# Attention stage: relu of the next queries at a unit's head, row norms before the tail scores, router set-up after unit 0, zero rows sent by SyncE

## Chip, cores and metric

One core of a Trainium2 chip runs one program. The metric is the device time of one execution in microseconds (us); the median of several runs counts. TensorE (PE), VectorE (DVE), ScalarE (ACT), GpSimd (POOL) and SyncE (SP) each work through a queue of their own in order; semaphores tie them together.

## What is computed

Attention with a compressive memory, whose output feeds a routed mixture of experts and then a dense one. Only the first is touched by the change.

```python
# attention: B, H, S, D = 4, 8, 576, 64
scores = q @ k.T / sqrt(D), causal;  a = softmax(scores)
local = a @ v
q_p = phi(q)            # phi(x) = max(x, 0) + min(exp(x), 1)
mem_out = (q_p @ M_prev) / (q_p . z_prev + 1e-6)
g = sigmoid(beta);  out = g * mem_out + (1 - g) * local
# routed experts: N = 2304 tokens, 512 wide, 8 experts, 1024 hidden
e_idx = argmax(x @ w_gate + modality_bias[modality_id])
out[t] = gate_w[t] * (relu(x[t] @ w1[e_idx]) @ w2[e_idx])
# dense experts: all 8 experts on all tokens, weighted by a Sinkhorn-normalised matrix
```

## The kernel before

**Units.** The function `attention` works in 16 units of two heads each (`NU = B * NP`, four units to a batch row). A unit's queries and keys are five tiles of up to 128 rows (`NT`), the last half full. The whole loop stands in a manual schedule (line 349): every engine gets its instructions in the order in which the loop emits them, and it does not pass one that waits. Two units overlap: in the pass for unit u the scores and exponentials of u are made, and the transposes, the memory product and the product with V of unit u-1 (`ex`); the keys and queries of u+1 are transposed there too (`nx`).

**The order of a pass** (lines 372 to 450). SP issues the loads of V of u+1 and of Q and K of u+2. Then `phi_a(u)`: VectorE forms phi of the queries (line 136), GpSimd multiplies it by z (line 137). `finish(u-1)`: the exponential of the tail scores of u-1 on ScalarE (line 262), two small VectorE steps (267, 268) and a scaling on GpSimd (269). `high(u)`: the scores of tiles 3 and 2 on TensorE (line 229) and their masks (336); these matmuls are called the head of the unit below. `top(u, 3)`: VectorE takes the row maxima (line 246). The transposed probabilities of u-1 are then evicted one bank after the other by VectorE and ScalarE (`ptrans`, lines 284 to 303), in between come `exps` (260), `keys` (188), `queries` (195, 196), `inverse` (175, 181), `low` (229, 345) and `phis` (203). After `ptrans(u-1, 3)` follow `ptrans` 6 and 7 (lines 298, 299, 303), `tails` (210 to 218), `last_scores`, the tail's maximum (248), `gate_v(u)` on GpSimd (144), the row norms `phi_b(u)` (VectorE 151 to 154, GpSimd 156), `phi_c(u)` (VectorE 161, 163, 166; GpSimd 165, 168), and `phi_0(u+1)`: relu of the next queries on GpSimd (line 127) and their exponential on ScalarE (128). Last come `memory(u-1)` (312) and `av(u-1)` (324), whose results VectorE writes to `xT` (326).

**Banks.** The transposes and the two products share four PSUM banks in turn (`ps_t`), so a product of `memory` needs the bank that `ptrans` 3 or 6 filled to be evicted. The scores have two buffers (`ps_s`): `low` needs the one of tile 3.

**Router.** `Router(...)` (line 358) sets up constants and loads the gate's weights, the modality ids and the bias; it runs after unit 0's queries and ahead of the loop. `pad_gate` (line 491) clears a tile on GpSimd and then has ScalarE's queue issue its load. `rt.batch(g)` is a generator: `some()` takes one step of it at three places of a pass. Its steps make the logits of a batch row's tokens, their maxima and one-hot rows, the row numbers, and send the rows to `xs_sorted` by indirect DMA from GpSimd.

**Zero rows.** `rt.clear()` (line 553) runs at the head of unit 2: GpSimd clears `zrow`, and ScalarE's queue issues 16 DMAs of 256 KB from it to `xs_sorted`.

Of the kernel before, what the change touches and what calls it, by code (L numbers as in the profile page):

```python
# [23 lines left out]
DVE_PT = (0, 1, 3)  # L24


def attention(ctx, tc, q, k, v, M_prev, z_prev, beta, xT, ident, router=None):
    nc = tc.nc
    es = ctx
    c1 = es.enter_context(tc.tile_pool(name="at_c", bufs=1))  # L30
# [89 lines left out]
                              src[b, 2 * a:2 * a + 2, 512:, :].rearrange("h p d -> p h d"))  # L120
            ld[u, nm] = t

    def phi_0(u):

        ex = tmp.tile([128, NT, 128], F32, tag="ex", name="ex")
        qp = tmp.tile([128, NT, 128], F32, tag="qp", name="qp")
        (nc.gpsimd if u else nc.vector).tensor_scalar(qp, ld[u, "q"], 0.0, None, ALU.max)
        nc.scalar.activation(ex, ld[u, "q"], AF.Exp)
        ph[u] = ex, qp

    def phi_a(u):

# [216 lines left out]
    with tc.manual_schedule():  # L349
        load(0, "kq")  # L350
        load_b(0)
        load(0, "v")
        load(1, "kq")
        keys(0)
        queries(0)
        tails(0, None)
        phi_0(0)
        rt = router and router()
        if rt:
            rt.ps, rt.busy = ps_t, busy  # L360
            rt.table_parts()

        back = iter(())

        def some():
            next(back, None)

        def finish(u):
            exps(u, 4)
            norm(u)  # L370

        for u in range(NU + 1):
            go, ex, nx = u < NU, u > 0, u + 1 < NU
            if nx:
                load(u + 1, "v")
            if u + 2 < NU:
                if (u + 2) % NP == 0:
                    load_b((u + 2) // NP)
                load(u + 2, "kq")
            if u == 2 and rt:  # L380
                rt.clear()
            if go:
                phi_a(u)
                if ex:
                    finish(u - 1)
                high(u)
                top(u, 3)
            some()
            if ex:
                ptrans(u - 1, 5)  # L390
                ptrans(u - 1, 4)
            if go:
                exps(u, 3)
            if ex:
                ptrans(u - 1, 0)
            if go:
                top(u, 2)
                exps(u, 2)
            if ex:
                ptrans(u - 1, 1)  # L400
            if nx and ex:
                keys(u + 1)
                queries(u + 1)
            if ex:
                inverse(u - 1)
            if go:
                low(u)
            if ex:
                ptrans(u - 1, 2)
                phis(u - 1)  # L410
            if go:
                top(u, 1)
                top(u, 0)
            if ex:
                ptrans(u - 1, 3)
            some()
            if ex:
                ptrans(u - 1, 6)
                ptrans(u - 1, 7)
            if go:  # L420
                exps(u, 1)
                exps(u, 0)
            if nx and not ex:
                last_scores(u)
                keys(u + 1)
                queries(u + 1)
            if nx or ex:
                tails(u + 1 if nx else None, u - 1 if ex else None)
            if go:
                if ex:  # L430
                    last_scores(u)
                top(u, 4)
                gate_v(u)
                phi_b(u)
                phi_c(u)
            some()
            if nx:
                phi_0(u + 1)
            elif go:
                finish(u)  # L440
            if ex:
                memory(u - 1, 0)
                memory(u - 1, 1)
                av(u - 1, 0)
                av(u - 1, 1)
                if rt and u % NP == 0:
                    for _ in back:
                        pass
                    back = rt.batch(u // NP - 1, ps_t)
                del un[u - 1]  # L450
        for _ in back:
            pass
# [46 lines left out]
class Router:  # L499
# [50 lines left out]
        self.tab = [c.tile([128, 4], I32, name=f"tab{i}") for i in range(2)]  # L550
        self.num = c.tile([1, 2], I32, name="num")

    def clear(self):
        nc = self.nc
        z = self.wk.tile([128, DM], F32, tag="zrow", name="zrow", bufs=1)
        nc.gpsimd.memset(z, 0.0)
        for e in range(NE):
            for r in range(TB // 128):
                nc.scalar.dma_start(self.xs[e * N + r * 128:e * N + (r + 1) * 128], z)

    def batch(self, g, ps):
        nc, xT, wk = self.nc, self.xT, self.wk
        tiles = GROUPS[g]
        t0, T = tiles[0], len(tiles)
        lt = []
        for c0 in range(0, T, 4):
            n = min(4, T - c0) * 128
            lq = ps.tile([128, 512], F32, tag="t", name="lq")
            for kd in range(KD):
                nc.tensor.matmul(lq[kd * 32:(kd + 1) * 32, :n], self.wg[:, kd],  # L570
                                 xT[:, kd, (t0 + c0) * 128:(t0 + c0) * 128 + n], start=True, stop=True)
            lt.append(wk.tile([128, 512], F32, tag="lt", name="lt"))
            nc.vector.tensor_copy(lt[-1][:, :n], lq[:, :n])
        yield
        L = wk.tile([128, T, NE], F32, tag="L", name="L")
        mx = wk.tile([128, T], F32, tag="mx", name="mx")
        ex = wk.tile([128, T, NE], F32, tag="ex", name="exr")
        gate = wk.tile([128, T], F32, tag="gate", name="gate")
        km = wk.tile([128, T], F32, tag="km", name="km")

        def bc(a):
            return a[:, :, None].to_broadcast([128, T, NE])

        def bce(a):
            return a[:, None, :].to_broadcast([128, T, NE])

        for c0 in range(0, T, 4):
            n = min(4, T - c0)
            lp = ps.tile([128, n, KD, 32], F32, tag="t", name="lp")
            for t in range(n):  # L590
                nc.tensor.transpose(lp[:, t].rearrange("p k e -> p (k e)"), lt[c0 // 4][:, t * 128:(t + 1) * 128],
                                    self.ident)
            nc.vector.tensor_reduce(L[:, c0:c0 + n], lp[:, :, :, :NE].rearrange("p t k e -> p t e k"), AX.X, ALU.add)
        nc.vector.tensor_tensor(L, L, self.bias[:, t0:t0 + T], ALU.add)
        nc.vector.tensor_reduce(mx, L, AX.X, ALU.max)
        nc.vector.tensor_tensor(L, L, bc(mx), ALU.subtract)
        nc.scalar.activation(ex, L, AF.Exp)
        yield
        nc.vector.tensor_reduce(gate, ex, AX.X, ALU.add)
        nc.vector.tensor_scalar(gate, gate, 1e-9, None, ALU.add)  # L600
        nc.vector.reciprocal(gate, gate)
        nc.vector.scalar_tensor_tensor(L, L, 0.0, bce(self.e8), ALU.is_ge, ALU.mult)
        nc.vector.tensor_reduce(km, L, AX.X, ALU.max)
        oh = self.oh[:, t0:t0 + T]
        nc.vector.tensor_tensor(oh, bc(km), bce(self.e8), ALU.is_equal)
        yield

        rp = ps.tile([128, T, NE], F32, tag="t", name="rp")
        nc.tensor.matmul(rp, self.ones, bce(self.base1), start=True, stop=False)
        nc.tensor.matmul(rp, self.ones, bce(self.cum), start=False, stop=False)  # L610
        nc.tensor.matmul(rp, self.tri, oh, start=False, stop=False)
        for t in range(T - 1):
            nc.tensor.matmul(rp[:, t + 1:], self.ones, oh[:, t:t + 1].to_broadcast([128, T - 1 - t, NE]), start=False,
                             stop=(t == T - 2))
        nc.vector.tensor_tensor(L, rp, oh, ALU.mult)
        nc.vector.tensor_reduce(self.rowf[:, t0:t0 + T], L, AX.X, ALU.add)
        nc.vector.tensor_copy(self.row[:, t0:t0 + T], self.rowf[:, t0:t0 + T])
        if g + 1 < len(GROUPS):
            for t in range(T):
                nc.vector.tensor_tensor(self.cum, self.cum, oh[:, t], ALU.add)  # L620
        for t in tiles:
            if t > t0 and t % 2:
                yield
            xp = ps.tile([128, DM], F32, tag="t", name="xp")
            for kd in range(KD):
                nc.tensor.transpose(xp[:, kd * 128:(kd + 1) * 128], xT[:, kd, t * 128:(t + 1) * 128], self.ident)
            xr = wk.tile([128, DM], F32, tag="xr", name="xr", bufs=6)
            nc.scalar.activation(xr, xp, AF.Copy, scale=gate[:, t - t0:t - t0 + 1])
            scatter(self.tc, self.moved, self.gap, self.xs[:, :], self.row[:, t:t + 1], xr)
# [770 lines left out]
```

## Time and profile before

| what | us |
|---|---|
| median of 3 runs | 2122.35 |
| the runs | 2119.94 to 2122.36 |
| the profiled execution, its own time | 2123.79 |
| span of its trace | 2122.1 |
| TensorE busy in the span | 2029.5 (96%) |
| VectorE, ScalarE, GpSimd busy | 1472.3, 853.0, 774.5 |
| mean granted TensorE clock | 0.981 |

The span is what lies between the first and the last instruction; 1.7 us of the execution lie around it. Busy shares are means over stages with different limits: the attention stage takes the first 322 us or so, and the expert stages the rest. A line of the timeline gives the start, the busy time, the engine, the source line, what is written from what, and in brackets how long the engine had been idle and what ended that.

### The profile page before, as it was taken

To read this page: it belongs to the slowest core of one execution; us is meant where nothing else is said; L and a number is where in the kernel's file an instruction comes from. 1 tells how busy PE (TensorE), PEld (TensorE's weight loads), DVE (VectorE), ACT (ScalarE), POOL (GpSimd) and SP (SyncE) were. 2 spreads that over 40 slices of the span, in tenths; PEclk is the share of its full clock that TensorE was granted. 3 is DMA by queue.
4 is the path that set the end of the run, shared out by engine and by line. 5 is a ranking of instruction groups with operands and counts; after the bars stand their busy time and mean duration, and the time that the engine had idled before them with its cause. 6 is when DMAs were issued, how large, how long until landed. Compare 5 with 4: busy or idle time off the path is not lost.

```text
span 2122.1 us, 31397 instructions
## 1 busy us (share of the span) xinstructions
PE 2029.5 (96%) x11478; PEld 1789.2 (84%) x11480; DVE 1472.3 (69%) x2538; ACT 853.0 (40%) x1792; POOL 774.5 (36%) x758
## 2 busy tenths in 40 slices
PE   5788889999989999999999999999999999999998
PEld 3556667999869998899889898899988999889997
DVE  4567666766668777776687677766778676777775
ACT  3454554655543433333343433333334333333332
POOL 4354541000024334344465433334347343333432
PEclk8899999999999999999999999999999999999999
DMA  4332206665632223443433212122122221212211
GB/s 97 111 78 59 75 26 224 201 214 195 202 122 65 60 80 60 63 77 60 75 65 100 70 60 80 60 69 71 60 78 92 70 70 60 79 60 71 70 60 40
DMA packets 238525, 187.36 MB, mean 88 GB/s; under 512 B 71444, under 2 KB 194324, under 8 KB 238356
## 3 DMA queue, kind: packets, MB, share of 16 engines
q1 hardware_dynamic: 229012, 171.48, 29.3%
q0 software_dynamic: 3520, 9.46, 1.2%
q10 hardware_dynamic: 5824, 4.25, 0.6%
q8 instruction: 95, 1.56, 0.3%
q14 instruction: 74, 0.61, 0.1%
HBM read 171.51 MB, written 13.64 MB: 87 GB/s over the span
## 4 chain that ended last, share of the span: by engine, by line
issue 30%; PE 24%; POOL 17%; DVE 0%; ACT 0%; POOLq 0%; DVEq 0%
PE y L1202 12%; PE prod L1131 11%; POOL T L1023 8%; POOL w1l L1017 7%; POOL out_dram L477 1%; PE lq L1243 0%; POOLq L1023 0%; POOL S L1101 0%; POOL S L1103 0%; POOL S L1102 0%; DVE w2l L1017 0%; POOL S4l L1017 0%; POOL S L1100 0%; PE lg L1255 0%; DVE c L1145 0%
## 5 line engine op out<-in xcount | busy, mean ns | idle before, releaser
L1149 ACT ACTIVATE hh<-c 128x384 fp32r<-128x384 f32 x384 | 202.0, 526 | 829.8 <-DVE c L1145 829.7
L1017 POOL TENSOR_TENSOR w1l<-T,w1h 128x1024 fp32r<-128x1024 f32 x94 | 226.7, 2411 | 842.4 <-ACT w1h L1017 842.4
L1202 PE MATMUL y<-w2h,hh 128*128 128x512 f32 x1152 | 453.3, 394 | 0.0
L1202 PE MATMUL y<-w2l,hh 128*128 128x512 f32 x1152 | 453.3, 393 | 0.0
L1202 PE MATMUL y<-w2h,hl 128*128 128x512 f32 x1152 | 452.6, 393 | 0.0
L1154 DVE SCALAR_TENSOR_TENSOR hl<-c,hh 128x384 fp32r<-128x384 f32 x384 | 418.1, 1106 | 1.1 <-ACT hh L1149 0.8
L1145 DVE TENSOR_TENSOR c<-prod,u 128x384 f32<-128x384 f32 x288 | 160.2, 556 | 155.6 <-PE prod L1131 152.7
L1202 PEld LDWEIGHTS y<-w2h,hh 128*128 128x128 f32 x1152 | 216.2, 188 | 32.8
L1202 PEld LDWEIGHTS y<-w2h,hl 128*128 128x128 f32 x1152 | 216.2, 188 | 28.5
L1202 PEld LDWEIGHTS y<-w2l,hh 128*128 128x128 f32 x1152 | 216.3, 188 | 27.9
L1023 POOL TENSOR_TENSOR T<-r,T 128x256 f32<-128x256 f32 x188 | 159.1, 846 | 14.8 <-issue 7.7
L1023 POOL TENSOR_TENSOR T<-r 128x256 f32<-128x256 f32 x188 | 161.1, 857 | 7.1
L1145 DVE TENSOR_TENSOR u<-prod,u 128x384 f32<-128x384 f32 x192 | 106.0, 552 | 58.1 <-PE prod L1131 57.7
L1145 DVE TENSOR_TENSOR u<-prod,p 128x384 f32<-128x384 f32 x96 | 53.5, 557 | 129.5 <-PE prod L1131 128.3
L1017 DVE TENSOR_TENSOR w2l<-r,w2h 128x512 fp32r<-128x512 f32 x188 | 137.1, 729 | 0.6 <-ACT w2h L1017 0.6
L1017 ACT CAST w2h<-r 128x512 fp32r<-128x512 f32 x188 | 106.7, 610 | 0.0
L1017 DVE TENSOR_TENSOR w1l<-r,w1h 128x512 fp32r<-128x512 f32 (+1 forms) x188 | 103.9, 553 | 0.0
L1145 DVE TENSOR_TENSOR c<-prod,p 128x384 f32<-128x384 f32 x96 | 53.5, 558 | 71.1 <-PE prod L1131 65.2
L1017 ACT CAST w1h<-T 128x1024 fp32r<-128x1024 f32 x94 | 97.0, 1032 | 1.0 <-POOL T L1023 1.0
L1159 ACT COPY p<-prod 128x384 f32<-128x384 f32 x96 | 46.1, 480 | 123.8 <-PE prod L1131 122.5
L1213 DVE SCALAR_TENSOR_TENSOR acc<-y,P,acc 128x512 f32<-128x512 f32 x126 | 92.4, 744 | 4.3 <-PE y L1202 4.3
L1017 ACT CAST w1h<-r 128x512 fp32r<-128x512 f32 (+1 forms) x188 | 94.5, 503 | 0.0
(387 smaller groups left out, 4179.2 us busy)
## 6 DMA issues: line engine op xcount, KB each, us to landing
r<-in_moe_w_dram SPq DMA_DIRECT2D x188, 512.0 KB, 4.1
r<-in_moe_w_dram SPq DMA_DIRECT2D x188, 256.0 KB, 2.9
xr<-xs_sorted SPq DMA_DIRECT2D x22, 256.0 KB, 5.0
kn<-in_k_dram SPq DMA_DIRECT2D x32, 128.0 KB, 2.6
qn<-in_q_dram SPq DMA_DIRECT2D x32, 128.0 KB, 2.8
vt<-in_v_dram SPq DMA_DIRECT2D x32, 128.0 KB, 2.7
xs_sorted<-zrow ACTq DMA_DIRECT2D x16, 256.0 KB, 3.7
zb<-in_z_prev_dram SPq DMA_DIRECT2D x4, 256.0 KB
```

Of the source, the lines that this page charges most:

```text
L477: i = tc.nc.gpsimd.indirect_dma_start(out=out, out_offset=bass.IndirectOffsetOnAxis(ap=idx, axis=0), in_=src, in_offset=None)
L1017: return (lambda: nc.scalar.copy(hi, src)), (lambda: eng.tensor_tensor(lo, src, hi.bitcast(F32), ALU.subtract))
L1023: sub = lambda i, a, b: (lambda: nc.gpsimd.tensor_tensor(T[:, i], a, b, ALU.subtract))
L1131: nc.tensor.matmul(p, a[:, kd], b[:, kd], start=(i == 0), stop=(i == 5))
L1145: nc.vector.tensor_tensor(st[o], a, st[b], ALU.add)
L1149: nc.scalar.activation(hh[:, f, a * HT:(a + 1) * HT], st[o], AF.Relu)
L1154: nc.vector.scalar_tensor_tensor(hl[:, f, w], st[o], 0.0, hh[:, f, w].bitcast(F32), ALU.max, ALU.subtract)
L1159: nc.scalar.copy(st["p1"], p)
L1202: nc.tensor.matmul(yt[t], a[:, f, t * 128:(t + 1) * 128], b[:, f], start=(j == 0 and f == 0 and i == 0), stop=(j == NJ - 1 and f == 1 and ...
L1213: nc.vector.scalar_tensor_tensor(acc[t], yt[t], P[:, m, e:e + 1], acc[t], ALU.mult, ALU.add)
```

## The change

Seven edits, all in the attention stage and its router. (1) The relu of the queries leaves `phi_0(u+1)` at the end of pass u and stands at the head of pass u, behind `gate_v(u)`; its buffer gets a third copy. (2) Exponential (`phi_e(u+1)`) and `phi_a(u+1)` stand at the end of pass u, `phi_a` thus no longer at the head of pass u+1. (3) `gate_v(u)` moves from the end of pass u to its head. (4) `phi_b(u)` moves from behind `top(u, 4)` to behind `ptrans(u-1, 3)`, ahead of `ptrans` 6. (5) `phi_e(u+1)` stands ahead of `top(u, 4)`. (6) The router is set up at the end of pass 0, behind `phi_a(1)`. (7) The 16 zero DMAs are issued by SP, eight each behind the loads of units 1 and 2. The generator `batch` has one more empty step ahead of the row numbers.

```diff
+    def relu(u):
+        qp = tmp.tile([128, NT, 128], F32, tag="qp", name="qp", bufs=3)
         (nc.gpsimd if u else nc.vector).tensor_scalar(qp, ld[u, "q"], 0.0, None, ALU.max)
-        nc.scalar.activation(ex, ld[u, "q"], AF.Exp)
+        ph[u] = tmp.tile([128, NT, 128], F32, tag="ex", name="ex"), qp
+    def phi_e(u):
+        nc.scalar.activation(ph[u][0], ld[u, "q"], AF.Exp)
...
-        phi_0(0)
-        rt = router and router()
-            rt.table_parts()
+        relu(0)
+        phi_e(0)
+        phi_a(0)
...
-            if u == 2 and rt:
-                rt.clear()
+            if 0 < u < 3:
+                rt.clear(u - 1)
             if go:
-                phi_a(u)
+                gate_v(u)
+            if nx:
+                relu(u + 1)
+            if go:
                 if ex:
                     finish(u - 1)
                 high(u)
...
             some()
+            if go:
+                phi_b(u)
             if ex:
                 ptrans(u - 1, 6)
                 ptrans(u - 1, 7)
...
+            if nx:
+                phi_e(u + 1)
+            if go:
                 top(u, 4)
-                gate_v(u)
-                phi_b(u)
                 phi_c(u)
             some()
             if nx:
-                phi_0(u + 1)
+                phi_a(u + 1)
             elif go:
                 finish(u)
+            if u == 0:
+                rt = router()
+                rt.ps, rt.busy = ps_t, busy
+                rt.table_parts()
...
-    def clear(self):
+    def clear(self, part):
-        for e in range(NE):
+        for e in range(NE // 2 * part, NE // 2 * (part + 1)):
             for r in range(TB // 128):
-                nc.scalar.dma_start(self.xs[e * N + r * 128:e * N + (r + 1) * 128], z)
+                nc.sync.dma_start(self.xs[e * N + r * 128:e * N + (r + 1) * 128], self.z)
...
         nc.vector.tensor_tensor(oh, bc(km), bce(self.e8), ALU.is_equal)
         yield
+        yield
```

## Rows read from the trace of the kernel before

**Rows 1.** Windows, head to head of units; columns as the second line says.

```profile
core 0: us, PE busy (x) PEld busy (x) DVE busy (x) ACT busy (x) POOL busy (x), PEclk, DMA share, GB/s
...
26.91:45.36 18.45, 14.59 (x98) 11.26 (x98) 10.93 (x30) 8.16 (x25) 8.31 (x7) 0.81 0.01 2
45.36:76.90 31.54, 15.25 (x107) 10.98 (x103) 10.91 (x27) 9.52 (x29) 8.73 (x8) 0.73 0.53 174
94.04:110.98 16.94, 14.61 (x107) 10.77 (x103) 11.17 (x28) 8.92 (x27) 8.25 (x8) 0.90 0.24 54
110.98:129.18 18.20, 16.24 (x119) 11.56 (x115) 12.14 (x30) 9.18 (x28) 8.23 (x7) 0.91 0.22 50
129.18:148.31 19.13, 15.83 (x128) 11.48 (x124) 15.57 (x46) 10.99 (x31) 12.04 (x14) 1.00 0.40 109
76.90:310.00 233.10, 196.57 (x1419) 143.92 (x1417) 158.64 (x404) 122.37 (x364) 121.50 (x117) 0.93 0.25 62
310.00:2122.00 1812.00, 1788.81 (x9806) 1615.53 (x9804) 1279.05 (x2051) 703.84 (x1350) 627.16 (x583) 1.00 0.32 90
```

**Rows 2.** Waits in 0 to 345 us: who for whom, sum, times, longest.

```profile
DVE qp L136 <- POOL qp L127: 39.1, 15, 4.5
ACT P L262 <- DMA xs_sorted<-zrow: 18.5, 1, 18.5
SPq L117 <- PE x L324: 176.7, 13, 21.3
```

**Rows 3.** Timeline of unit 4, head at 94.04: start, us, engine, operation, idle before.

```profile
92.42 0.81 DVE L151 TENSOR_REDUCE nrm<-ex 128x10 f32<-128x640 f32 x1
...
93.81 0.17 DVE L161 TENSOR_SCALAR su<-su 128x8 f32<-128x8 f32 x1
...
94.38 0.81 DVE L326 TENSOR_TENSOR xT<-x,R 128x256 f32<-128x256 f32 x2
...
98.93 1.21 DVE L246 TENSOR_REDUCE nm<-s 128x2 f32<-128x1024 f32 x1
...
105.39 0.56 DVE L284 COPY pt<-tp 128x384 f32<-128x384 f32 x1 [0.40 <-PE tp L283]
...
106.39 0.21 DVE L213 COPY pT<-tl 128x64 f32<-128x64 f32 x1
...
106.98 1.22 PE L312 MATMUL x<-pT,Mb 128*128 128x256 f32 x4
```

**Rows 4.** Timeline of unit 2: the zero rows, its late head, its maxima.

```profile
50.10 11.75 ACTq L559 DMA_DIRECT2D xs_sorted<-zrow  x16
...
62.78 1.65 PE L229 MATMUL s<-kT,qTp 64*128 64x384 f32 x4 [16.29 <-ACT P L262]
...
64.80 1.23 DVE L246 TENSOR_REDUCE nm<-s 128x2 f32<-128x1024 f32 x1 [1.69 <-PE s L336]
```

**Rows 5.** Timeline of units 0 and 1, up to unit 1's phi.

```profile
8.75 0.53 ACTq L514 DMA_DIRECT2D ids<-in_moe_modality_id_dram  x1
...
9.31 0.40 PE L336 MATMUL s<-mk,idb 128*128 128x128 bf16 x4
...
13.06 0.18 DVE L519 CAST idf<-ids 128x18 f32<-128x18 int32 x1 [3.81 <-DMA ids<-in_moe_modality_id_dram]
...
15.95 2.09 DVE L246 TENSOR_REDUCE nm<-s 128x2 f32<-128x1024 f32 x2
16.00 1.53 POOL L137 TENSOR_TENSOR ex<-qp,zb 128x640 f32<-128x640 f32 x1 [8.91 <-DMA vt<-in_v_dram]
...
27.99 0.61 POOL L165 COPY rr<-rc 128x512 f32<-128x512 f32 x1
...
28.56 1.05 POOL L168 TENSOR_TENSOR qp<-qp,nrm 128x512 f32<-128x512 f32 x1
...
31.47 0.83 DVE L136 SCALAR_TENSOR_TENSOR qp<-ex,qp 128x640 f32<-128x640 f32 x1 [3.52 <-POOL qp L127]
```

**Rows 6.** Two VectorE operations by tile: duration ns min/median/max, first and last start.

```profile
L166 DVE TENSOR_TENSOR nrm<-nrm,su x16: 116/330/334, 27.6 to 310.6; 128x8 f32<-128x8 f32 x16
L1154 DVE SCALAR_TENSOR_TENSOR hl<-c,hh x384: 532/591/2551, 616.1 to 2106.0; 128x384 fp32r<-128x384 f32 x192
```

More of the change, by code (lines that the diff above doesn't have):

```diff
@@ L24, with attention @@
 DVE_PT = (0, 1, 3)
-def attention(ctx, tc, q, k, v, M_prev, z_prev, beta, xT, ident, router=None):
+def attention(ctx, tc, q, k, v, M_prev, z_prev, beta, xT, ident, router):
     nc = tc.nc
@@ L121, in load @@
             ld[u, nm] = t
-    def phi_0(u):
-        ex = tmp.tile([128, NT, 128], F32, tag="ex", name="ex")
-        qp = tmp.tile([128, NT, 128], F32, tag="qp", name="qp")
+    def relu(u):
+        qp = tmp.tile([128, NT, 128], F32, tag="qp", name="qp", bufs=3)
         (nc.gpsimd if u else nc.vector).tensor_scalar(qp, ld[u, "q"], 0.0, None, ALU.max)
-        nc.scalar.activation(ex, ld[u, "q"], AF.Exp)
-        ph[u] = ex, qp
+        ph[u] = tmp.tile([128, NT, 128], F32, tag="ex", name="ex"), qp
+    def phi_e(u):
+        nc.scalar.activation(ph[u][0], ld[u, "q"], AF.Exp)
     def phi_a(u):
@@ L356, in attention @@
         tails(0, None)
-        phi_0(0)
-        rt = router and router()
-        if rt:
-            rt.ps, rt.busy = ps_t, busy
-            rt.table_parts()
+        relu(0)
+        phi_e(0)
+        phi_a(0)
+        rt = None
         back = iter(())
@@ L445, in attention @@
                 av(u - 1, 1)
-                if rt and u % NP == 0:
+                if u % NP == 0:
                     for _ in back:
@@ L551, in __init__ @@
         self.num = c.tile([1, 2], I32, name="num")
-    def clear(self):
+    def clear(self, part):
         nc = self.nc
-        z = self.wk.tile([128, DM], F32, tag="zrow", name="zrow", bufs=1)
-        nc.gpsimd.memset(z, 0.0)
-        for e in range(NE):
+        if part == 0:
+            self.z = self.wk.tile([128, DM], F32, tag="zrow", name="zrow", bufs=1)
+            nc.gpsimd.memset(self.z, 0.0)
+        for e in range(NE // 2 * part, NE // 2 * (part + 1)):
             for r in range(TB // 128):
-                nc.scalar.dma_start(self.xs[e * N + r * 128:e * N + (r + 1) * 128], z)
+                nc.sync.dma_start(self.xs[e * N + r * 128:e * N + (r + 1) * 128], self.z)
     def batch(self, g, ps):
```

## The prediction

> **What bounds the kernel now.** I read the windows first. From 310 us on TensorE is busy for 1788.81 of 1812.00 us at full clock [rows 1], and nothing of the change reaches there: I carry that part over unchanged. Ahead of it TensorE is not the limit: units 3 to 15 take 233.10 us with 196.57 us of TensorE work, at a mean clock of 0.93 [rows 1]. A plain unit, without router work, takes 16.94 us with 14.61 us of TensorE at a clock of 0.90; at full clock that work would be some 13.1 us (14.61 x 0.90), my estimate. Then I read the waits: 15 times VectorE stands before phi (line 136) for GpSimd's relu, 39.1 us in all or 2.6 us a unit, and ScalarE stands once for 18.5 us behind the zero rows [rows 2]. The timeline shows why the first of these is on the path: in unit 4 the maxima of tile 3 start 4.89 us behind the head (98.93 against 94.04) [rows 3], and everything of the unit hangs on them: evictions, exponentials, the free score buffer. In unit 2, where the stall had let relu and phi pass before the head, they start 2.02 us behind it (64.80 against 62.78), waiting for the masks alone [rows 4].
>
> **A plain unit.** (Edits 1 to 5.) The relu goes to GpSimd's queue most of a unit earlier, and phi to the end of the pass before. VectorE's next work at the head is the maxima, at about head + 2.05 us (2.02 in unit 2). From there to the copy of the tail bank (line 213) unit 4 takes 7.46 us (98.93 to 106.39) [rows 3]. The norms now come in between: 1.39 us (92.42 to 93.81) [rows 3]. Of the gaps that VectorE had in this stretch 0.40 us stands ahead of the third eviction [rows 3]; with a maximum that starts earlier against the same TensorE order I close it and, by estimate, as much again: the smaller gaps ahead of the low tiles. So 7.46 + 1.39 - 0.78 = 8.07 us. From line 213 to the next head unit 4 takes 4.59 us (106.39 to 110.98) [rows 1, 3]. The first half of the memory product (0.6 of the 1.22 us of line 312 [rows 3]) no longer has to stand behind that, since its bank is the one of the third eviction: 4.0 us. Sum: 2.05 + 8.07 + 4.0 = 14.1 us.
>
> What is late next? First VectorE's end of the pass. The norms leave it (1.39 us), phi comes (0.83 us [rows 5]); the copies to `xT` ended at head + 1.15 us (94.38 + 0.81) [rows 3], so about 0.55 us remain to head + 2.05 (0.35 us of that I give to the two small steps of `finish`, which have room from the 0.56 us by which phi is shorter). Second, GpSimd: from the reciprocals at the end of a pass until the tail's scaling it has 7.85 us of work in a row (8.25 us busy a unit [rows 1], less some 0.4 for the early piece of the norms), and the tail's transposes want it at about head + 7.7 us: it fits with little over. Third, ScalarE: 8.92 us a unit [rows 1], no limit.
>
> A price that the trace of before does not show is that of phi (two inputs in SBUF) beside GpSimd's copy of the reciprocals and its scaling (0.61 and 1.05 us [rows 5]): before, phi ran when GpSimd had just finished its relu. Between nothing and both of them, 1.66 us, I take one, 0.61 us: line 166, the nearest row, has two such inputs and takes 0.33 us at the median against 0.116 at best [rows 6], so it is held, but by one instruction of GpSimd and not by a row of them. With the slack above that is 0 to 0.2 us on VectorE and, since GpSimd then starts its next piece 0.8 us late, about 0.3 us a unit in all. **14.4 us a plain unit**, with ends at 13.6 (TensorE's 13.1 and one wait) and 15.3 (phi held by both: 14.1 + 1.66 - 0.55 of slack, and 0.1 for GpSimd).
>
> The Trainium skill bears on this place. SBUF — State Buffer, section Who interferes with whom, says that a VectorE instruction with two SBUF inputs and a GpSimd instruction that reads SBUF take one port by turns, and that the second to issue blocks fully. The trace agrees in line 1154: 0.59 us at the median, 2.55 at the longest [rows 6]. By that rule alone, with GpSimd issuing first both times, a unit would be the 15.3 us of the upper end.
>
> **Router pieces.** Units 5 and 6 carry one batch: VectorE has 12.14 and 15.57 us of work against 11.17 in unit 4 [rows 1], together 5.4 us more. The one-hot part stays at the end of a pass, where there is a little room; the logits and the row numbers lie between the maxima and line 213, on the path. The empty step shifts the row numbers from a head to mid-pass and the last scatters into the following unit, whose tail scaling they delay. I take 4.9 us a batch, three batches: 14.7 us, give or take 5.
>
> **Units 3 to 15.** 13 x 14.4 + 14.7 = 201.9 us against 233.1: **31.2 us saved**.
>
> **Unit 2.** (Edit 7.) Its 31.54 us [rows 1] hold the stall: the zeros occupy ScalarE's queue for 11.75 us and its next exponential waits 18.5 us, with the head 16.29 us behind [rows 2, 4]. On SP they stand behind the loads of their unit, and the loads of the next unit wait for `av` anyway (13 waits, 176.7 us [rows 2]): eight DMAs, about 5.9 us of issue by half of 11.75, fit into that wait. If that cover were gone, the next loads would start up to 6 us late, once or twice, for data wanted a unit later. So unit 2 becomes a plain unit: 31.54 - 14.4 = **17.1 us saved**.
>
> **Units 0 and 1.** (Edit 6.) The maxima of unit 0 start at 15.95 us although its masks end at 9.71 [rows 5]: the set-up stands ahead of them. They can start at 10.0, some 5.9 us earlier. But the set-up now stands at the end of pass 0, in three queues. GpSimd's scaling, which ended at 29.61 (28.56 + 1.05), ends 5.9 us for the earlier start and 1.4 for the norms sooner, at 22.3; the product with z follows (1.53 us): 23.8; only then comes `pad_gate`'s memset, for which ScalarE's queue waits, with the ids behind it. Their load takes 4.31 us from issue to VectorE's cast (8.75 to 13.06), so the cast is at about 28.8, and VectorE's set-up (2 us) ends near 30.9. The maxima of unit 1 stand behind it: 31.0 us, against about 32.5 before (31.47 and phi's 0.83, then two small steps) [rows 5]. So of 5.9 us about 1.5 are left, less 0.2 for the norms on a colder clock: **1.3 us saved**, between 2 us lost (bias landing late) and 6 saved (nothing held).
>
> **Sum.** 31.2 + 17.1 + 1.3 = 49.6 us. On the profiled execution's own time: 2123.8 - 49.6 = 2074.2. That execution is 1.4 us above the median of the runs, so for the median: **2072.8 us**.
>
> **Rivals.**
> (a) GpSimd and its port set the pace. Phi is held by both GpSimd pieces in each unit, the tail scaling comes late: 15.3 us a unit, 14 x 0.9 = 12.6 us less saved, 2085. For it: 7.85 us in a row, and line 1154's longest of 2.55 us [rows 6]. Against it: GpSimd is idle for half of a unit. 0.15. (It is what the rule of the Trainium skill above, SBUF — State Buffer, gives.)
> (b) More is saved. TensorE no longer pauses, its clock stays at 2.4 GHz, units come to 13.6 us (14 x 0.8 = 11.2 us), and the set-up holds nobody (4.7 us): 2057. For it: a unit without the pause has no half-clock stretch behind it. Against it: VectorE has 11.17 us of work a unit and sits in the chain of almost every step. 0.15.
> (c) The edit does not do what it says: VectorE's wait at the head only moves to the norms ahead of the tail's evictions, the period stays near 16.8, and only unit 2's stall goes: 2122.4 - 17 = 2105. Against it: the wait was for GpSimd's relu (2.6 us), the norms are 1.39 us of work. 0.06.
> (d) Slower. The place is the wait for the tail's banks ahead of the memory product: if TensorE's clock fell to 1.2 GHz there and stayed low through the unit, each us of its 13.1 us of work would take one more. From 18.4 us a unit on (16.94, and the 18.4 us saved in units 0 to 2 spread over 13 units) the kernel would be slower than before; at 20 us a unit it is 2144 (13 x 3.06 us more, 18.4 less). Against it: mean clock 0.90 with a wait of over 2 us in each unit [rows 1]. 0.02.
>
> **How the numbers follow.** My forecast has 0.62. Its own spread is -11 to +13 us for the plain unit, 5 for the router, -5 to +3 for units 0 and 1, not all at one end: 2058 to 2088, which takes in (a) and nearly all of (b). Outside are (c) and (d) and half of (b). A measurement of this kernel can tell about 0.2% from no change, 4 us. Faster by more than that: all but (d), 0.97; within it 0.01; slower 0.02.
>
> **What would show it.** In the trace after: no wait of phi for the relu; the maxima at head + 2 us; plain units of 14 to 15 us; no wait of the tail's exponential for `zrow`, eight zero DMAs each in two passes of SP; VectorE waiting for the ids near 25 to 29 us; phi at times longer than 0.83 us. The prediction is wrong if plain units stay above 15.5 us, if TensorE's clock falls in them, or if unit 1's head comes earlier than 25 us.

## The result and the profile after

The changed kernel takes 2069.94 us (median of four runs, 2068.15 to 2073.20) against 2121.89 us: ratio 0.976, 95% interval 0.974 to 0.978, 52 us faster. The forecast was 2072.8 us. The span of the trace falls from 2122.1 to 2068.2 us.

Windows of the changed kernel, head to head: units 2, 4, 5 and 6, then units 3 to 15 together. Compare [rows 1].

```profile
core 0: us, PE busy (x) PEld busy (x) DVE busy (x) ACT busy (x) POOL busy (x), PEclk, DMA share, GB/s
44.52:58.41 13.89, 13.30 (x107) 9.56 (x103) 10.85 (x28) 8.76 (x28) 8.71 (x8) 1.00 0.72 218
72.28:86.17 13.89, 13.31 (x106) 9.55 (x103) 10.85 (x28) 8.76 (x28) 8.71 (x8) 1.00 0.29 65
86.17:102.07 15.90, 14.93 (x119) 10.18 (x115) 12.23 (x34) 8.93 (x29) 8.71 (x8) 1.00 0.25 58
102.07:120.42 18.35, 15.38 (x124) 10.96 (x120) 14.37 (x41) 10.52 (x31) 11.40 (x13) 1.00 0.33 85
58.41:259.70 201.29, 185.41 (x1438) 131.43 (x1434) 153.14 (x407) 120.24 (x365) 126.09 (x118) 1.00 0.29 74
```

A plain unit now takes 13.89 us, 16.94 before, and TensorE is busy for 13.31 of them at a granted clock of 1.00 (0.90 before). So TensorE itself is nearly the bound. Units 5 and 6, which carry router work, take 2.0 and 4.5 us more. Unit 2 is a plain unit. The second half of unit 1's first scores is later than before (29.14 against 26.91 us), yet unit 2's head is 0.84 us earlier (44.52 against 45.36). The first half of them (tile 3) starts at 19.31 us, 24.16 before.

One line of the trace of before belongs here, the first TensorE work behind the last unit's products, and its counterpart after:

```profile
312.04 0.87 PE L290 MATMUL tp<-ident,P 128*128 128x128 f32 x6
```

```profile
259.69 0.88 PE L292 MATMUL tp<-ident,P 128*128 128x128 f32 x6
```

The last unit of before ended at 312.04 us, not at the 310.00 at which the forecast cut. With this the sum closes: units 0 and 1 gave 0.8 us (37.75 to 36.98), unit 2 gave 17.65 (31.54 to 13.89), units 3 to 15 gave 33.9 (235.14 to 201.28), and what follows up to the end 1.5. That is 53.9 us, the difference of the spans.

Timeline of unit 4 after, head at 72.28. Compare [rows 3].

```profile
71.74 0.82 DVE L138 SCALAR_TENSOR_TENSOR qp<-ex,qp 128x640 f32<-128x640 f32 x1
71.92 1.10 POOL L167 COPY rr<-rc 128x512 f32<-128x512 f32 x1 [3.40 <-DVE nrm L168]
...
72.28 1.77 PE L231 MATMUL s<-kT,qTp 64*128 64x512 f32 x8
...
74.31 1.23 DVE L248 TENSOR_REDUCE nm<-s 128x2 f32<-128x1024 f32 x1 [0.77 <-PE s L338]
...
76.72 1.80 POOL L126 TENSOR_SCALAR qp<-qn 128x640 f32<-128x640 f32 x1
...
80.39 0.81 DVE L153 TENSOR_REDUCE nrm<-ex 128x10 f32<-128x640 f32 x1
...
81.78 0.42 DVE L300 COPY pt<-tp 128x256 f32<-128x256 f32 x1
...
82.31 0.21 DVE L215 COPY pT<-tl 128x64 f32<-128x64 f32 x1
...
84.34 0.23 DVE L220 TENSOR_SCALAR qTp<-tl 64x64 f32<-64x64 f32 x1 [1.69 <-ACT qTp L219]
```

Phi (L138) now runs ahead of the head and waits for nobody; the maxima (L248) start 2.03 us behind the head, waiting for the masks alone. The relu (L126) runs in mid-unit, where nobody wants it yet. Two things stand in the last lines that experiments below come back to: the norms (L153) stand in front of the tail's evictions (L300), and VectorE is idle for 1.69 us a little later (before L220).

Four of the waits after (0 to 293 us; who for whom, sum, times, longest): the two at the head of unit 1 and two of TensorE's in the units behind it. Compare [rows 2]:

```profile
PE s L231 <- ACT P L264: 8.7, 1, 8.7
...
ACT P L264 <- POOL ix L659: 7.5, 1, 7.5
...
PE x L314 <- DVE qTp L220: 3.3, 3, 1.1
...
PE tp L298 <- POOL P L271: 3.0, 5, 0.6
```

No wait for the relu is left (39.1 us before), and none for the zero rows (18.5 us). The first two lines are one event, at the head of unit 1 behind the router's set-up. The last is the wait of TensorE for GpSimd's scaling of the tail, 0.58 us in unit 4: it is all the time that TensorE stands there.

### The profile page after: what moved, and what is told of

It is laid out like the page before. It is cut to its first block, busy times and chain, and to the rows that moved or that the text cites. A ratio compares the mean times of both kernels' runs of the same rounds, so it can differ in the third digit from the quotient of the medians.

```text
span 2068.2 us, 31414 instructions
## 1 busy us (share of the span) xinstructions
PE 2014.2 (97%) x11480; PEld 1773.1 (86%) x11480; DVE 1465.9 (71%) x2538; ACT 850.2 (41%) x1792; POOL 780.6 (38%) x758
## 4 chain that ended last, share of the span: by engine, by line
issue 31%; PE 24%; POOL 17%; DVE 0%; ACT 0%; POOLq 0%; DVEq 0%
PE y L1214 13%; PE prod L1143 11%; POOL T L1035 8%; POOL w1l L1029 7%; POOL out_dram L487 1%; PE lq L1255 0%; POOLq L1035 0%; POOL S L1113 0%; POOL S L1115 0%; POOL S L1114 0%; DVE w2l L1029 0%; POOL S4l L1029 0%; POOL S L1112 0%; PE lg L1267 0%; DVE c L1157 0%
```

## The experiments

Each is the changed kernel with one edit, except e11 and e9, which combine. For every run the ratio is to the kernel before. Edits 3 and 5 were not taken back alone. What e1 to e4 lose (18, 48, 5 and 6 us) adds up to more than the 52 us gained, so these are not shares of it.

**e1: the zeros back on ScalarE's queue, all sixteen in unit 2.**

```diff
-            if 0 < u < 3:
-                rt.clear(u - 1)
+            if u == 2:
+                rt.clear(0)
+                rt.clear(1)
...
-                nc.sync.dma_start(self.xs[...], self.z)
+                nc.scalar.dma_start(self.xs[...], self.z)
```

> The changed kernel, with all 16 zero DMAs issued by ScalarE's queue at the head of unit 2 again. My theory: the queue was the whole of that stall, 31.54 us for unit 2 against 13.89 after the change, so unit 2 comes back to some 31 us and the kernel to about 2087 us (2070 and 17). Rival: the transfers themselves cost the time wherever they are issued (landing 3.7 us each beside other loads), and the changed order of relu and phi saved most of unit 2: then no more than 6 us, 2076.

2087.69 us, ratio 0.984 [0.982, 0.986]: 17.75 us slower than the changed kernel. Timeline of unit 2 (its head begins at 44.20, the next one at 74.98):

```profile
47.94 11.52 ACTq L571 DMA_DIRECT2D xs_sorted<-zrow  x16
59.51 0.74 ACT L264 ACTIVATE P<-s,nm 128x576 f32<-128x576 f32 x1 [16.53 <-DMA xs_sorted<-zrow]
...
60.39 1.65 PE L231 MATMUL s<-kT,qTp 64*128 64x384 f32 x4 [15.06 <-ACT P L264]
```

The stall of [rows 4] is back, and the unit takes 30.78 us. So the step "unit 2 becomes a plain unit" holds, and the zeros on SP cost nothing that can be seen: 4.49 us of issue in unit 1 and 5.61 in unit 2 there, inside SP's wait for `av`.

**e2: the relu back at the end of the pass, phi back behind the head.** The other edits stay.

```diff
-            if nx:
-                relu(u + 1)
             if go:
                 if ex:
+                    phi_a(u)
...
             if nx:
-                phi_a(u + 1)
+                relu(u + 1)
+                phi_e(u + 1)
```

> The changed kernel, with relu and exponential of the next queries at the end of a pass and phi at the head of the next again; the norms stay ahead of the tails. My theory: the relu's place is worth most of a plain unit's 3 us. GpSimd then goes from the reciprocals through 0.61, 1.05 and 1.81 us before phi can start, which ends about 2.2 us behind where VectorE could begin the maxima: plain units near 16.1 us (13.89 now), a clock below 1.00 in them, some 30 us in all, about 2100 us. Rival: the norms' move did it by taking 1.39 us out of the same end of the pass; then plain units stay below 14.9 us and the kernel below 2084.

2118.48 us, ratio 0.998 [0.997, 0.999], 48 us slower than the changed kernel. The plain units are not alike: 17.92, 18.09 and 18.73 us in units 2 to 4, 16.93 us in units 8 and 12. Windows of units 4 and 8:

```profile
80.47:99.20 18.73, 16.15 (x106) 12.19 (x102) 12.08 (x27) 8.96 (x28) 8.26 (x8) 0.82 0.21 48
156.13:173.06 16.93, 13.50 (x106) 9.54 (x102) 11.91 (x27) 8.77 (x28) 8.29 (x8) 1.00 0.23 53
```

Timeline behind the head of unit 4 (80.47):

```profile
81.73 1.81 POOL L126 TENSOR_SCALAR qp<-qn 128x640 f32<-128x640 f32 x1
...
83.51 1.25 POOL L146 TENSOR_TENSOR vt<-vt,om 128x640 f32<-128x640 f32 x1
83.58 1.87 DVE L138 SCALAR_TENSOR_TENSOR qp<-ex,qp 128x640 f32<-128x640 f32 x1 [2.49 <-POOL qp L126]
...
87.57 1.09 PE L177 MATMUL rp__996<-ident,rr 128*128 128x128 f32 x4 [2.58 <-DVE pt L286]
```

The direction is the theory's, the size is not. The wait for the relu is 2.49 us, as before; then phi itself takes 1.87 instead of 0.82 us, since GpSimd's `gate_v` has started 0.07 us ahead of it; TensorE stands for 2.58 us, and the four transposes behind that take 1.09 us, which take 0.60 in the changed kernel. Unit 8 has the same phi (1.88 us) and the same wait (2.61 us), but keeps a granted clock of 1.00: the late phi costs 3.0 us there (16.93 against 13.89). The other 1.8 us of unit 4 come with its clock of 0.82; why it fell there and not in unit 8 is not shown. With phi late, the changed order is thus no better than the old one in a plain unit (16.94 us before). Of the 14.5 us by which unit 3's head is ahead of the kernel before (62.38 against 76.90), 6.6 are left at the first routed matmul (338.65 against 345.27). The move of the relu, with phi behind it, carries the change.

**e3: the norms back behind the tail's maximum.**

```diff
-            if go:
-                phi_b(u)
             if ex:
                 ptrans(u - 1, 6)
...
                 top(u, 4)
+                phi_b(u)
                 phi_c(u)
```

> The changed kernel, with the norms behind the tail's maximum again. My theory: a plain unit is held by GpSimd's row of work from the reciprocals to the tail scaling, which would start 1.39 us later with one more piece of 0.46 us in it, while the evictions of the tail get 1.39 us earlier of which about 0.8 counts: 13.89 + 1.0 = 14.9 us a plain unit, some 14 us in all, 2084 us. Rival: VectorE's own row alone sets the unit; its work is the same in either order, and it now waits 0.77 us at the head, so the time stays at 2070 or falls by up to 10 us.

2075.38 us, ratio 0.978 [0.976, 0.980]: 5.4 us slower, where 14 was forecast. Units 3, 4 and 12 take 14.7 us, near the forecast 14.9; unit 8 takes 13.11, behind a unit 7 of 17.68 us at a granted clock of 0.90 (14.51 at 1.00 in the changed kernel). But units 5, 9 and 13, which carry the first pieces of a batch, take 14.7, 15.4 and 14.7 us, where they took 15.9, 16.5 and 15.9. Up to unit 15's head 4.2 us are lost in all (250.39 against 246.21). So the order of the norms is worth 0.8 us in a plain unit; e8 shows that neither of the two places is the best one.

**e4: the router's set-up in front of the loop, as before the change.**

```diff
-        rt = None
+        rt = router()
+        rt.ps, rt.busy = ps_t, busy
+        rt.table_parts()
```

> The changed kernel, with the router set up ahead of the loop again. My theory: behind pass 0 the set-up costs about what it saves, since ScalarE's queue waits for GpSimd's memset and VectorE for the ids: unit 1's scores of tile 2 start at 29.14 us, later than the 26.91 before the change. In front, unit 0 loses 5.8 us again, but unit 1 becomes a plain unit right behind it: unit 2 starts near 41 us instead of 44.52, the kernel is about 3 us faster, 2067. Rival: the edit is worth the 5.9 us by which unit 0's maxima got earlier; then 2076.

2075.70 us, ratio 0.978 [0.976, 0.979]: 5.8 us slower, where I had expected a gain. Timeline of VectorE ahead of unit 0's maxima:

```profile
15.69 0.52 DVE L527 CAST idf<-ids 128x18 f32<-128x18 int32 x1 [5.51 <-DMA ids<-in_moe_modality_id_dram]
...
18.83 2.09 DVE L248 TENSOR_REDUCE nm<-s 128x2 f32<-128x1024 f32 x2
```

In the kernel before the maxima began at 15.95 us [rows 5]. Here the set-up stands behind phi's product with z on GpSimd, its loads go out later, and VectorE's small steps run beside GpSimd. The position alone is not what counts, but what GpSimd does ahead of it and beside it. Of the 5.8 us, however, only 1.3 are lost at the front (unit 2's head at 45.80 against 44.52). Units 6 and 10 lose 4.0: they take 19.84 and 20.12 us, against 18.35 and 17.56, at granted clocks of 0.91 and 0.92 instead of 1.00. Window of unit 6:

```profile
103.36:123.20 19.84, 16.85 (x124) 11.62 (x120) 14.48 (x41) 10.53 (x31) 12.67 (x15) 0.91 0.30 78
```

That the time is the rival's 2076 is luck.

**e5: without the empty step of the router's batch.**

```diff
         nc.vector.tensor_tensor(oh, bc(km), bce(self.e8), ALU.is_equal)
         yield
-        yield
```

> The changed kernel without the empty step ahead of the row numbers. In the changed kernel units 6, 10 and 14 take 18.35, 17.56 and 18.61 us against 13.89 for a plain one. My theory: the empty step puts two row transposes in front of the memory products, whose banks then come free only with VectorE's tail copy (waits of 1.06 and 1.08 us). Without it these units lose that, but the row numbers wait for the one-hot rows at the head: about 1 us a batch, 3 us in all, 2067. Rival: the wait at the head costs as much or more (1.2 us of TensorE and 1.6 us of VectorE on the path of the maxima): 2070 to 2074.

2068.44 us, ratio 0.975 [0.973, 0.976]; 1.5 us by the medians, 2.8 by the spans, which is below what a measurement can tell. Unit 6 falls from 18.35 to 17.39 us, unit 10 rises from 17.56 to 18.92. The empty step is worth nothing either way.

**e6: the copy of the reciprocals on ScalarE.**

```diff
-        nc.gpsimd.tensor_copy(rr.rearrange(...), rc[...])
+        nc.scalar.copy(rr.rearrange(...), rc[...])
```

> The changed kernel, with the copy of the reciprocals (1.10 us on GpSimd beside phi) on ScalarE instead. My theory: GpSimd is not the bound of a plain unit; TensorE's wait of 0.58 us for the tail scaling goes, but the tail's eviction still stands behind the norms on VectorE: 13.89 us within 0.2, kernel 2070 within 3. Rival: GpSimd and its port set the pace; then a plain unit falls by 0.6 us or more, 8 us in all, 2061.

2071.80 us, ratio 0.976 [0.975, 0.978]; plain units 13.97 us. GpSimd has 0.6 us less to do in each unit (8.08 busy instead of 8.71), its scaling no longer stands behind a held copy, and TensorE's wait for the tail's scaling is gone; in its place TensorE waits 0.46 us for VectorE's copy of the tail bank, and the unit doesn't shorten. GpSimd is not the bound, and rival (a) falls. The plain units show this and not the kernel's time: units 6 and 10 take 19.50 and 19.80 us here, at a granted clock of 0.91.

**e7: the set-up split.** GpSimd's part and the loads in front of the loop, VectorE's work on ids and bias (`prepare`) at the end of pass 2.

```diff
+        rt = router()
+        rt.ps, rt.busy = ps_t, busy
+        rt.table_parts()
         phi_a(0)
-        rt = None
...
-            if u == 0:
-                rt = router()
...
+            if u == 2:
+                rt.prepare()
```

> The changed kernel, with the router's loads, memsets and constants ahead of the loop (loads behind unit 0's exponential on ScalarE's queue) and only VectorE's bias work later, at the end of pass 2. My theory: nothing then holds units 0 and 1: unit 1's scores of tile 2 start near 21 us instead of 29.14, unit 2 near 35.5 instead of 44.52: 9 us saved, 2061. Rival: units 0 and 1 are held by the first loads and the cold clock, and the set-up fills their gaps: less than 3 us, 2067 or more.

2072.64 us, ratio 0.976 [0.975, 0.978]. Unit 3's head is at 50.57 us, 7.8 earlier than in the changed kernel, and then unit 3 takes 20.21 us, at a granted clock of 0.83. Units 10 and 14 take 4.4 us more than in the changed kernel (20.32 and 20.27 us, at 0.92). Timeline at its head, VectorE and GpSimd alone:

```profile
51.28 1.04 POOL L170 TENSOR_TENSOR qp<-qp,nrm 128x512 f32<-128x512 f32 x1
51.38 0.97 DVE L562 TENSOR_SCALAR is<-idf 128x18 f32<-128x18 f32 x1
52.28 1.53 POOL L139 TENSOR_TENSOR ex<-qp,zb 128x640 f32<-128x640 f32 x1
52.38 1.59 DVE L563 TENSOR_TENSOR biasn<-is,bias 128x144 f32<-128x144 f32 x1
53.77 1.31 POOL L146 TENSOR_TENSOR vt<-vt,om 128x640 f32<-128x640 f32 x1
54.01 1.11 DVE L562 TENSOR_SCALAR is<-idf 128x18 f32<-128x18 f32 x1
55.06 1.80 POOL L126 TENSOR_SCALAR qp<-qn 128x640 f32<-128x640 f32 x1
55.15 0.78 DVE L563 TENSOR_TENSOR b<-is,bias 128x144 f32<-128x144 f32 x1
55.97 0.31 DVE L565 TENSOR_TENSOR biasn<-biasn,b 128x144 f32<-128x144 f32 x1
```

Steps of 0.2 to 0.3 us (in e10, below) take 1.0 to 1.6 us. Each of the first three ends when the GpSimd instruction that began just ahead of it ends (52.35 against 52.32, 53.97 against 53.81, 55.12 against 55.08), and then GpSimd's next one starts first again. The last two don't: they take 0.78 and 0.31 us and end at 55.93 and 56.28, while GpSimd's relu, which began ahead of both, runs until 56.86.

**e10: the same split, `prepare` in VectorE's idle time of unit 2.** Its place is behind VectorE's two copies of the tail bank (L215, L218), ahead of the wait for ScalarE's `qTp`.

```diff
             nc.scalar.activation(qt[0:64, 512:576], p[0:64, 64:128], AF.Copy, scale=0.125)
+            if now == 2:
+                rt.prepare()
```

> The router's set-up is split as in e7 (its GpSimd copies and its loads ahead of unit 0, its VectorE bias work later), but the bias work now stands in unit 2 right behind the evictions of the next tile's q, where VectorE waits for TensorE's pass of the memory and phi of the next unit. Theory: e7 gained 7.8 us at the heads of units 1 to 3 and lost them again because the bias work stood at the end of a pass beside GpSimd's pieces and pushed VectorE's next unit; in a place where VectorE idles it costs little. Then unit 3 takes within 1 us of a plain unit (13.9) and the time is 2070 - 7.8 = 2062, between 2059 and 2065. Rival: the cast and the small multiplies are stretched wherever they stand beside GpSimd, unit 3 or unit 2 is again over 18 us and the time 2070 or more.

2066.91 us, ratio 0.974 [0.973, 0.976]. Timeline of VectorE in unit 2:

```profile
47.81 0.18 DVE L562 TENSOR_SCALAR is<-idf 128x18 f32<-128x18 f32 x1
48.02 0.31 DVE L563 TENSOR_TENSOR biasn<-is,bias 128x144 f32<-128x144 f32 x1
```

The same instructions take 0.18 and 0.31 us, where GpSimd is idle, and units 2 and 3 take 13.89 and 13.88 us. So the place is right, and unit 3's head stays 7.2 us ahead (51.21 against 58.41). But the kernel gains 3.0 us, not the forecast 7.8. Of the 7.2 us, 4.4 are lost in two units with router work, unit 10 (20.31 against 17.56 us) and unit 14 (20.27 against 18.61). Windows of the product with V in unit 10, here and in the changed kernel:

```profile
174.30:178.50 4.20, 4.20 (x29) 2.50 (x28) 1.24 (x4) 1.18 (x3) 3.65 (x6) 0.67 0.03 13
```

```profile
180.00:182.90 2.90, 2.90 (x29) 1.85 (x28) 1.45 (x6) 1.51 (x4) 2.23 (x4) 1.00 0.00 0
```

The product with V behind the memory takes 4.2 us at a granted clock of 0.67 here, against 2.9 at 1.00. In both kernels TensorE has just stood twice, 1.32 and 1.09 us here, 0.77 and 1.08 there. Why the clock fell behind the one and not behind the other stays open; unit 6 of the changed kernel has waits of 1.06 and 1.08 us in this place and kept 1.00, unit 6 of e4 has 1.07 and 1.09 and did not. e7 loses in the same two units, e4 and e6 in units 6 and 10: that loss comes with none of these edits alone.

**e8: the norms in the same idle time of VectorE, in every unit.** They leave their place ahead of the tail's evictions.

```diff
-            if go:
-                phi_b(u)
             if ex:
                 ptrans(u - 1, 6)
...
             nc.scalar.activation(qt[0:64, 512:576], p[0:64, 64:128], AF.Copy, scale=0.125)
+            if now is not None:
+                phi_b(now)
...
+        elif now is not None:
+            phi_b(now)
```

> The changed kernel, with the norms placed in VectorE's wait for ScalarE's tail copy (1.69 us in each unit) instead of ahead of the tail's evictions. My theory: that wait is the one gap of VectorE that takes the 1.39 us for nothing; the evictions come 1.39 us earlier, and GpSimd's row (tail scaling) becomes the bound: a plain unit falls from 13.89 to about 13.4 us, 6 us in all, 2064. Rival: GpSimd already is the bound, its early piece of the norms now comes just ahead of its copy of the reciprocals: 13.9 us or more, 2070 or more.

2056.73 us, ratio 0.969 [0.967, 0.970]: 13 us faster than the changed kernel, more than forecast. Windows of a plain unit, and its timeline:

```profile
70.62:83.86 13.24, 13.24 (x107) 9.63 (x103) 10.97 (x28) 8.77 (x27) 8.85 (x9) 1.00 0.30 68
```

```profile
79.27 0.21 DVE L215 COPY pT<-tl 128x64 f32<-128x64 f32 x1
...
79.53 0.81 DVE L153 TENSOR_REDUCE nrm<-ex 128x10 f32<-128x640 f32 x1
...
81.30 0.23 DVE L222 TENSOR_SCALAR qTp<-tl 64x64 f32<-64x64 f32 x1 [0.30 <-ACT qTp L219]
```

VectorE's idle time ahead of L222 shrinks from 1.69 to 0.30 us, TensorE has no idle time left in the unit (so it, and not GpSimd's row as forecast, is the bound; plain units take 13.1 to 13.3 us), and the router's units gain too (unit 6: 16.84 instead of 18.35 us).

**e11: e8 and e10 together.**

> e8 (normaliser's steps behind the next tile's q evictions) and e10 (bias work there too, once, in unit 2) together. Theory: the two save at different places, the one in each plain unit, the other at the heads of units 1 to 3: 2056.7 - 7.8 = 2049. Rival: they use up the same idle time of VectorE in unit 2, or what the front saves is given back later: 2053 or more.

2052.15 us, ratio 0.967 [0.966, 0.969]. By the medians that is 4.6 us from e8, and the intervals overlap (0.9655 to 0.9687 against 0.9671 to 0.9703). The traces say more: the first routed matmul starts at 274.4 us, at 280.5 in e8 and at 292.8 in the changed kernel. Unit 3's head is 7.9 us ahead of e8's, and 1.5 of that go in unit 3, where GpSimd's scaling of the tail comes late. Windows of unit 3 (units 2 and 4 take 13.1 us), and the line in it:

```profile
49.65:64.29 14.64, 13.29 (x106) 9.54 (x102) 12.32 (x32) 9.60 (x29) 9.81 (x9) 1.00 0.44 114
```

```profile
58.47 0.66 PE L304 MATMUL tp<-ident,P 128*128 128x128 f32 x4 [1.34 <-POOL P L277]
```

The runs (2049.72 to 2052.34 us) lie between the 2049 us of the theory and the 2053 of the rival, and the times don't tell the two apart; the trace stands nearer to the theory, 6.1 of 7.8 us kept up to the routed experts.

**e9: e11 without the empty step.**

> As e11, and without the empty step between a router batch's transposes and its row products (e5's edit, which alone brought 1.5 us). Theory: e11 less 1.5 to 2.8: 2047, between 2043 and 2051. Rival: the empty step's place was filled with the waits that e8 takes away, and the edit is worth nothing any more: e11's own time or more, 2049 and above.

2053.21 us, ratio 0.968 [0.966, 0.969], and the first routed matmul at 274.8 us: no difference from e11. The rival holds.

## Why the prediction was right, step by step

**The plain unit, 14.4 forecast, 13.89 measured.** Its three stretches came out one by one: head to maxima 2.03 us (forecast 2.05), maxima to the copy of the tail bank 8.00 (74.31 to 82.31; forecast 8.07), from there to the next head 3.86 (82.31 to 86.17; forecast 4.0). The first of them is partly luck: the 2.02 us behind it were counted from 62.78 us [rows 4], which is only the second half of unit 2's head (its first half began at 45.36) at a granted clock of 0.50; a whole head at 1.00 takes as long. What was wrong is the 0.3 us on top for phi beside GpSimd. Phi takes 0.82 us in all units, just as before. The price exists but is paid by the other side: GpSimd's copy of the reciprocals, 0.61 us before [rows 5], takes 1.10 us in most units, and e6 shows that the unit is no shorter without it. I had let GpSimd start first. The timeline suggests why it doesn't: phi is VectorE's next instruction behind the step (L168) to which the trace puts the copy's release, and starts at 71.74, the copy at 71.92.

The Trainium skill says in SBUF — State Buffer, section Who interferes with whom, that it is the order of issue that decides who blocks. Three places here agree: phi first, and the copy takes 1.10 us (changed kernel); `gate_v` first by 0.07 us, and phi takes 1.87 us (e2); GpSimd first each time, and three of VectorE's small steps end with its instructions (e7). One place does not: beside GpSimd's relu, which began first, VectorE's steps with two inputs take 0.78 and 0.31 us and don't wait for its end (e7; 0.31 us in unit 1 of the changed kernel too), so the order alone does not settle it. The prediction used the rule with the order the wrong way round.

**The router, 14.7 forecast, 20.7 measured** (201.3 - 13 x 13.89). The first batch adds 2.0 + 4.5 + 0.6 us to units 5 to 7; units 9 to 11 pay 7.3 us, units 13 and 14 pay 6.7. I had priced VectorE's extra work and left out TensorE, which is nearly the bound of the unit by then. Its own work is the larger part: in these eight units it is busy 13.6 us longer than in eight plain ones (1.6 and 2.1 us in units 5 and 6), of the 21.1 us that they take more. Another 5.9 us are waits in units 6, 10 and 14: the row transposes go through the banks of `ps_t` ahead of the memory product, and the second four of them and the second half of the product each wait for an eviction. TensorE in unit 6:

```profile
114.66 0.66 PE L638 MATMUL xp<-ident,xT 128*128 128x128 f32 x4 [1.06 <-DVE pt L305]
115.15 0.60 PE L314 MATMUL x<-pT,Mb 128*128 128x256 f32 x2
116.83 0.81 PE L314 MATMUL x<-pT,Mb 128*128 128x320 f32 x2 [1.08 <-DVE qTp L220]
```

The two errors cancel: 13 x 0.5 = 6.6 us too much in the plain units, 6.0 too little for the router, and units 3 to 15 take 201.3 us where 201.9 was forecast. That this term is right to 0.6 us is thus partly luck. The saving was forecast as 31.2 us and is 33.9; the other 2.0 us of the difference come from the end of the stretch before, cut at 310.00 instead of 312.04 us.

**Unit 2: 17.65 us, forecast 17.1.** Right, and shown by e1. The half of a microsecond is the plain unit's.

**Units 0 and 1: 0.8 us, forecast 1.3.** The chain was the one forecast, each link somewhat later. Timeline of the set-up after:

```profile
25.15 0.20 POOL L504 MEMSET wg<- 128x128 f32 x1
...
28.25 0.74 ACT L264 ACTIVATE P<-s,nm 128x576 f32<-128x576 f32 x1 [7.48 <-POOL ix L659]
...
29.56 0.51 DVE L529 CAST idf<-ids 128x18 f32<-128x18 int32 x1 [7.33 <-DMA ids<-in_moe_modality_id_dram]
...
32.77 1.20 DVE L248 TENSOR_REDUCE nm<-s 128x2 f32<-128x1024 f32 x1
```

The memset came at 25.15 us (forecast 23.8), the cast at 29.56 (28.8), the maxima of unit 1 at 32.77 (31.0). At the front, VectorE reached the tail's maximum of unit 0 4.9 us earlier than before (20.39 against 25.24) and not 5.9, and GpSimd's copy was held (1.08 us instead of 0.61); at the end, VectorE's steps were stretched (the cast 0.51 us instead of 0.18 [rows 5]). What I had not named is the queue that is held: the loads of weight, ids and bias stand on ScalarE ahead of the tail's exponential, which waits 7.5 us, and the second half of unit 1's head, 8.7 us, behind it. The first half starts at 19.31 us: by the letter that is the sign of being wrong that the prediction named last (before 25 us), but [rows 1] and the sum count from the second half, which came at 29.14.

**The rivals.** (a) falls with e6. (b) came true in its reason, the clock at 1.00 in plain units, and these came nearer to its 13.6 us than to the forecast of 14.4 (13.89); its sum did not come true, since the router takes back what the plain units give and the set-up still holds unit 1. (c) falls: the wait is gone. (d) did not come true in the changed kernel; e2 shows that its direction exists, but not in every unit: behind a wait of 2.6 us on TensorE units 2 to 4 take 17.9 to 18.7 us at clocks of 0.82 to 0.91, units 8 and 12 behind the same wait 16.93 us at 1.00.

## What to carry to other kernels

Look for the place of a step by who is idle there: the norms cost 0.6 to 0.8 us a unit in front of an eviction and nearly nothing some instructions later, in a wait that the same engine has anyway (2069.9 to 2056.7 us), and small VectorE steps want a stretch in which GpSimd is idle too. When work is moved, follow each queue that it is moved onto, its DMA issues included, and ask of two instructions that hinder each other which one starts first. Price added work on the engine that will be the bound after the change. In an experiment, compare units as well as times: e4, e7 and e10 lost 4.0 to 4.4 us in units that their edits did not touch. Check a sum term by term against the new trace even where the total is right: here two errors of some 6 us hid each other.

## What was not expected of the hardware

A VectorE step of 128x18 elements, 0.18 us with GpSimd idle (e10), took 0.97 and 1.11 us when a GpSimd instruction with two inputs had begun ahead of it (e7); the cast and the five steps behind it take 1.6 us in e10 (47.61 to 49.23) and 5.5 us in e7 (50.76 to 56.28). For three of these steps the end of GpSimd's instruction, not their own length, sets the price; beside GpSimd's relu, with one input, it does not (0.78 and 0.31 us), and why is not shown.

And behind waits of TensorE that differ by 0.01 us, 1.06 and 1.08 us in unit 6 of the changed kernel, 1.07 and 1.09 in unit 6 of e4, the same product with V takes 2.92 us at a granted clock of 1.00 in one and 3.76 us at 0.77 in the other, a mean of the two levels of 2.4 and 1.2 GHz; in unit 10 of e10 it is 4.2 us at 0.67. Why is open.
